# Band scores of two heads from one product over 128 partitions

## The chip, the cores and the metric

The kernel runs on one core of one Trainium2 chip. The metric is the device time of one launch in microseconds (us). An engine's name is shortened as in the profile: PE is TensorE (PEld its weight loads), DVE is VectorE, ACT is ScalarE, POOL is GpSimd and SP is SyncE, which issues most of the DMAs. Engines run their own instructions in order and wait for one another by semaphores.

## The reference

A local-global attention over 8 batches, 8 heads, 576 positions of 64 values, followed by a mixture of 16 experts on its output. The part that the change touches is the local attention: a position attends to the positions less than 4 away, a band of 7.

```python
def _attn_ref(q, k, v):
    B, H, S, D = q.shape                       # 8, 8, 576, 64
    factor = 4
    scale = 1.0 / np.sqrt(D)
    ...
    q_d = q.reshape(B, H, S // 4, factor, D).mean(axis=3)   # and k_d, v_d
    out_d = sm_attn(q_d, k_d, v_d)
    out_up = np.repeat(out_d, factor, axis=2)
    pos = np.arange(S)
    mask = np.abs(pos[:, None] - pos[None, :]) < factor
    scores = scale * np.matmul(q, k.transpose(0, 1, 3, 2))
    scores = np.where(mask, scores, -1000000000.0)
    scores = scores - np.max(scores, axis=-1, keepdims=True)
    attn = np.exp(scores)
    attn = attn / (np.sum(attn, axis=-1, keepdims=True) + 1e-09)
    out_local = np.matmul(attn, v)
    return (out_up + out_local).astype(np.float32)

def reference(**kwargs):
    ...
    attn_out = _attn_ref(**attn_kwargs)
    B, H, S, D = attn_out.shape
    x = np.ascontiguousarray(attn_out.transpose(0, 2, 1, 3)).reshape(B * S, H * D)
    return _moe_ref(x=x, **moe_kwargs)         # a group of 4, then an expert of 4 in it, for each token
```

## The kernel before

The attention works in 16 units. A unit is two heads of two batches: the 128 partitions hold the 64 values of the one head and the 64 of the other, and the free dimension holds the two batches and the positions. `load_k` (L177) and `load_q` (L181) bring them in that form, a DMA each on SP's queue, into `kt` (three buffers, made in `__init__`, L76) and `qT`; keys are padded by 3 positions at both ends on the host.

Band scores: 576 positions of a batch are 18 blocks of 32 queries, and a block sees 38 keys. `s_local` (L239) issues, for one head `h`, 36 float32 products (18 blocks of two batches): 64 partitions of that head, 32 queries as the stationary side, 38 keys as the moving side, into one of four column groups `j` and one of nine places `g` of a PSUM bank [128, 9, 38]. In the first three units (`EARLY_UNITS`) a bf16 product with the identity first puts the mask there. The profile shows two matmul records, and two weight loads, to a float32 product.

`s_local_out` (L256) then takes that bank, for one head: DVE adds the mask (L268) and takes the maximum per row (L269), POOL subtracts it (L270); in the first three units DVE takes the maximum (L265) and subtracts (L266). The result goes to `E` [128, 9, 48, 2], whose last index is the head. `s_local_exp` (L272) takes the exponential on ACT, again for one head. `soft_local_sum` and `soft_local` (both heads at once) divide by the sums; `turn_e` turns `E` for the product with the windows of values, `x_bank` (L419).

The global half reads the same `kt`: `pool_k` (L228) sums each four keys, on DVE with one reduction over [128, 2, 144, 4] or on POOL with three adds, as its step says, into `kd`; `pool_q` does the same for the queries. `s_down` (L290) multiplies them, and `s_down_max`, `s_down_exp`, `soft_down`, `turn_pd`, `out_down`, `turn_down`, `down_store` and `load_down` lead its result to the windows `vw`, from which `x_bank` adds both halves. PSUM for scores has three banks (pool `psd`), for the rest four (`ps`).

After the attention, logits and the router (`logits`, `choose`, `places`, `lists`, `ranks`) find each token's expert. One early expert is computed while the last units end; the others follow in `Experts.main`.

The order is written out by hand. `ORDER`, a string of steps such as `s_local 9 0` or `pool_k 7 P`, is run through in order, and each engine and each DMA queue gets its instructions in that order. Which engine takes a step with a choice is the step's last letter (D for DVE, P for POOL, A for ACT, S for SP). `pool_k` is on DVE in units 0, 1, 3, 5, 6, 8 and 10, on POOL in the nine others. The steps at the start are:

```
shared_rows; warm_up 12; masks; masks_out A; load_k 1; clear E 1; s_local 0 1; clear_windows 0; pool_q 0 D
pool_k 0 D; clear E 0; load_q 1; s_local 0 0; s_local_out 0 1; quarter_sum; clear vs 0; s_local_out 0 0; load_k 2
```

Before these stand the loads and memsets of `__init__`. `shared_rows` copies a pattern to two buffers on DVE (the copies have the helper's line, L161); `clear_windows` (L139) clears a buffer of `vw` on POOL, `clear` (L109) the rims of `E` (L114) and a part of `vs` (L116).

Of the kernel before, what the change touches and what calls it, by code (L numbers as in the profile page):

```python
# [9 lines left out]
F32 = mybir.dt.float32  # L10
# [4 lines left out]
ALU = mybir.AluOpType  # L15
AX = mybir.AxisListType
# [3 lines left out]
P = 128  # L20
B, H, S, D = 8, 8, 576, 64
SD = S // 4
G = 9
W = 38
WW = 48
LEAD = (WW - W) // 2
NBLK = 18
# [20 lines left out]

KEYS = (0, 112, 160)

TILES = (slice(0, P), slice(160, 160 + P), slice(112, 176))


class Attention:
# [9 lines left out]
    def __init__(self, tc, q, k, v, idf, xd, left, right, dram):  # L64
        nc = self.nc = tc.nc
        self.tc, self.q, self.k, self.idf = tc, q, k, idf
        n = NTOK * DM
        self.v, self.vm = v[0:n].rearrange("(b h s d) -> b h s d", h=H, s=S, d=D), v[n:].rearrange("(u p f) -> u p f", u=4 * NB, p=SD)
        cp = self.cp = left.enter_context(tc.tile_pool(name="attc", bufs=1))
        self.a1 = left.enter_context(tc.tile_pool(name="att1", bufs=1))  # L70
        self.a2 = left.enter_context(tc.tile_pool(name="att2", bufs=2))
        self.inp = right.enter_context(tc.tile_pool(name="inp", bufs=2, side="right"))
        self.odd = [dram.tile([320, P], F32, name=f"odd{i}") for i in range(2)]
        self.st, self.banks, self.lg = {}, {}, {}
        self.xd = xd
        self.kt = [self.inp.tile([P, 2, S + 6], F32, name=f"kt{i}", bufs=1) for i in range(3)]  # L76
        self.load_k(0)
        self.load_q(0)
        self.mask = self.inp.tile([P, G, W], BF16, name="mask", bufs=1)
        self.vw = [(cp.tile([P, 2 * NBLK, P], F32, name=f"vw{i}") if i < 2 else self.inp.tile([P, 2 * NBLK, P], F32, name="vw2", bufs=1)) for i in range(3)]  # L80
        self.warm = self.inp.tile([P, 4 * P], BF16, name="warm", bufs=1)
        nc.vector.memset(self.warm, 0.0)
        one = cp.tile([1, 1], F32, name="one")
        nc.gpsimd.memset(one, 0.0)
        nc.scalar.activation(one, one, AF.Exp)
        self.idb = cp.tile([P, P], BF16, name="idb")
        self.vd = [cp.tile([P, 3, 2, D], F32, name=f"vd{i}") for i in range(2)]
        self.vs = [self.inp.tile([P, 3, 2, 4 * D], F32, name=f"vs{i}", bufs=1) for i in range(3)]
        self.mg = [cp.tile([P, 5], F32, name=f"mg{i}") for i in range(2)]
        self.sg = [cp.tile([P, 5], F32, name=f"sg{i}") for i in range(2)]  # L90
        self.rg = [cp.tile([P, 6], F32, name=f"rg{i}") for i in range(2)]
        self.kept = {}
        for n, more, shape in (
            ("pt", 1, [P, G * P]), ("x", 2, [P, G, P]), ("PdT", 1, [P, 3, 2 * SD]), ("od", 1, [P, 2 * SD]), ("odn", 1, [P, 3, 2, D])
        ):
            self.kept[n] = [cp.tile(shape, F32, name=f"{n}0")] + [self.inp.tile(shape, F32, name=f"{n}{i + 1}", bufs=1) for i in range(more)]
        self.E = [cp.tile([P, G, WW, 2], F32, name=f"E{i}") for i in range(2)]
        self.xT = cp.tile([P, 27 * P // 2], F32, name="xT")
        self.edge = self.inp.tile([P, 3, W], F32, name="edge", bufs=1)
# [9 lines left out]
    def clear(self, what, i):  # L109

        memset = self.nc.gpsimd.memset
        if what == "E":
            for w in (slice(0, LEAD), slice(LEAD + W, WW)):
                memset(self.E[i][:, :, w], 0.0)  # L114
        elif what == "vs":
            memset(self.vs[i][:, 2], 0.0)  # L116

    def masks(self):

        nc = self.nc  # L120
        m, me = self.edge[:, 0], self.edge[:, 1:3]
        nc.gpsimd.memset(m, 0.0)
        for j in range(4):
            s = m[32 * j : 32 * j + 32]
            for sign, base in ((1, 0), (-1, 6)):
                nc.gpsimd.affine_select(out=s, in_=s, pattern=[[sign, W]], compare_op=ALU.is_ge, fill=-1e30, base=base, channel_multiplier=-sign)
        for i, (sign, base) in enumerate(((1, -3), (-1, 34))):
            nc.gpsimd.affine_select(out=me[:, i], in_=m, pattern=[[sign, W]], compare_op=ALU.is_ge, fill=-1e30, base=base, channel_multiplier=0)
# [45 lines left out]
            self.st[u] = {"h0": 2 * hp, "b0": 2 * bp}  # L174
        return self.st[u]

    def load_k(self, u):  # L177
        self.unit(u)
        self.nc.sync.dma_start(out=self.kt[u % 3], in_=self.k[u])

    def load_q(self, u):  # L181
        s = self.unit(u)
# [43 lines left out]
    def pool_k(self, u, eng):  # L226
        s = self.st[u]
        kd = s["kd"] = self.inp.tile([P, 2, SD], F32, tag="kd", name=f"kd{u}")  # L228
        x = self.kt[u % 3][:, :, 3 : 3 + S].rearrange("p b (s t) -> p b s t", t=4)
        if eng == "D":  # L230
            self.nc.vector.tensor_reduce(out=kd, in_=x, axis=AX.X, op=ALU.add)
        else:
            self.add4(kd, [x[:, :, :, t] for t in range(4)])

    def pool_v(self, u):
        x = self.vs[u % 3].rearrange("p k b (t d) -> p k b t d", t=4)
        self.add4(self.vd[u % 2], [x[:, :, :, t] for t in range(4)])

    def s_local(self, u, h):  # L239

        nc = self.nc
        s = self.st[u]
        pt = self.bank(("s", h), u, [P, G, W], True)
        early = u < EARLY_UNITS
        if early:
            nc.tensor.matmul(pt.rearrange("p g w -> p (g w)"), self.idb, self.mask.rearrange("p g w -> p (g w)"), start=True, stop=False, skip_group_check=True)
        r = slice(64 * h, 64 * h + 64)
        for lin in range(2 * NBLK):
            g, j = divmod(lin, 4)
            b, blk = divmod(lin, NBLK)  # L250
            nc.tensor.matmul(
                pt[32 * j : 32 * j + 32, g], s["qT"][r, b, 32 * blk : 32 * blk + 32], self.kt[u % 3][r, b, 32 * blk : 32 * blk + W], start=not early, stop=True,
                skip_group_check=True,
            )

    def s_local_out(self, u, h):  # L256
        nc = self.nc
        s = self.st[u]
        pt = self.banks.pop((("s", h), u))
        if "ml" not in s:  # L260
            s["ml"] = self.a2.tile([P, G, 2], F32, tag="ml", name=f"ml{u}")
            s["sl"] = self.a2.tile([P, G, 2], F32, tag="sl", name=f"sl{u}")
        m, e = s["ml"][:, :, h], self.E[u % 2][:, :, LEAD : LEAD + W, h]
        if u < EARLY_UNITS:
            nc.vector.tensor_reduce(out=m, in_=pt, axis=AX.X, op=ALU.max)  # L265
            nc.vector.tensor_tensor(out=e, in0=pt, in1=m.unsqueeze(2).to_broadcast([P, G, W]), op=ALU.subtract)  # L266
        else:
            nc.vector.tensor_tensor(out=e, in0=pt, in1=self.mask, op=ALU.add)  # L268
            nc.vector.tensor_reduce(out=m, in_=e, axis=AX.X, op=ALU.max)  # L269
            nc.gpsimd.tensor_tensor(out=e, in0=e, in1=m.unsqueeze(2).to_broadcast([P, G, W]), op=ALU.subtract)  # L270

    def s_local_exp(self, u, h):  # L272
        e = self.E[u % 2][:, :, LEAD : LEAD + W, h]
        self.nc.scalar.activation(e, e, AF.Exp, scale=SCALE)

    def vec(self, e):
# [114 lines left out]
    def turn_down(self, u):  # L391
        pt = self.bank("odt", u, [P, 3, P])
        for c, q in enumerate(TILES):
            n = q.stop - q.start
# [810 lines left out]
shared_rows; warm_up 12; masks; masks_out A; load_k 1; clear E 1; s_local 0 1; clear_windows 0; pool_q 0 D  # L1205
pool_k 0 D; clear E 0; load_q 1; s_local 0 0; s_local_out 0 1; quarter_sum; clear vs 0; s_local_out 0 0; load_k 2
load_q 2; pool_q 1 P; load_v 0; s_down 0; warm_up 6; s_down_max 0; s_local_exp 0 1; s_down_exp 0 0; s_local_exp 0 0; s_down_exp 0 2
s_down_exp 0 1; pool_q 2 D; pool_k 1 D; s_local 1 1; clear_windows 1; s_local_out 1 1; s_local 1 0; clear vs 2; turn_pd 0 0
soft_local_sum 0 D; turn_pd 0 2; s_local_out 1 0; load_k 3; turn_pd 0 1; turn_pd_out 0 1 A; turn_pd_out 0 0 A; soft_local 0
turn_pd_out 0 2 A; s_down 1; s_local_exp 1 0; pool_v 0; out_down 0; s_local_exp 1 1; turn_e 0 0; s_down_max 1; clear vs 1  # L1210
turn_e 0 2; s_down_exp 1 0; soft_down 0 P; s_down_exp 1 1; load_windows 0; turn_e 0 1; soft_local_sum 1 D; turn_e_out 0 2 A
# [214 lines left out]
```

## Time and profile before

| | us |
|---|---|
| three timed runs | 752.67, 755.56, 758.88 |
| their median | 755.56 |
| the profiled execution | 760.53 |
| its span, first to last instruction | 758.7 |
| PE busy | 701.6 |
| DVE busy | 462.4 |
| ACT busy | 362.7 |
| POOL busy | 266.0 |

The busy times are sums over the whole span; the mean granted clock of TensorE was 0.964. Matmuls overlap, so a mean duration of one is longer than its share of the time. A row of the profile names the line, the engine, the operation and "output<-inputs"; "idle before, releaser" is the time in which the engine had nothing to run before these instructions, and what ended it. "issue" means that the engine waited for nothing that the profile shows.

### The profile page before, as it was taken

The page shows a single profiled execution, that of the slowest core. Times are in us where ns is not written, and L with a number is a line of the kernel's source. Part 1 is how long each engine was busy: PE and PEld are TensorE (multiplying, and loading weights), DVE is VectorE, ACT ScalarE, POOL GpSimd, SP SyncE. Part 2 cuts the span into 40 slices and gives each one's busy share as a digit, 9 for nine tenths or more (in the row PEclk, how much of TensorE's full clock was granted, in tenths as well). Part 3 has the DMA queues.
Part 4 walks back from the last instruction along what each step waited for, and adds up shares of the span by engine and source line. Part 5 has one row for each costly group of instructions (what it writes and reads, how often), then busy time and mean ns, then how long its engine had stood idle before and what let it go on. Part 6 is the DMA issues. An engine that isn't in the chain of part 4 may idle for free. (4 is left out here: it accounts for less than half of the span.)

```text
span 758.7 us, 19970 instructions
## 1 busy us (share of the span) xinstructions
PE 701.6 (92%) x8132; PEld 638.7 (84%) x8133; DVE 462.4 (61%) x834; ACT 362.7 (48%) x797; POOL 266.0 (35%) x307
## 2 busy tenths in 40 slices
PE   7788878897887878999999999999999999999996
PEld 4666757686665767999899999999999999999985
DVE  7877775898685583764545454555555555565541
ACT  3436534665564423654445444444545455555531
POOL 8966664676462552102130312203113113212211
PEclk9889998999989999999999999999999999999999
DMA  8779899789869535674463555555556556656600
GB/s 296 249 193 282 239 265 278 219 219 255 214 163 256 156 111 165 212 228 167 153 191 115 191 175 172 185 168 193 188 190 204 184 193 210 202 201 195 220 26 25
DMA packets 158243, 146.94 MB, mean 194 GB/s; under 512 B 69396, under 2 KB 129812, under 8 KB 158148
## 3 DMA queue, kind: packets, MB, share of 16 engines
q1 hardware_dynamic: 133540, 115.11, 50.8%
q0 software_dynamic: 7088, 21.66, 8.2%
q10 hardware_dynamic: 17520, 8.85, 4.4%
q8 instruction: 65, 1.06, 0.6%
q14 instruction: 30, 0.25, 0.1%
HBM read 124.29 MB, written 22.29 MB: 193 GB/s over the span
## 5 line engine op out<-in xcount | busy, mean ns | idle before, releaser
L863 PE MATMUL ph<-xh,w1h 128*128 128x256 f32 (+13 forms) x512 | 162.3, 318 | 0.0
L834 POOL DMA_INDIRECT xg<-xd,gi x47 | 48.5, 1032 | 319.1 <-ACT yo L937 289.7
L863 PE MATMUL ph<-xl,w1h 128*128 128x256 f32 (+13 forms) x512 | 157.0, 308 | 0.0
L863 PE MATMUL ph<-xh,w1l 128*128 128x256 f32 (+13 forms) x512 | 156.8, 308 | 0.0
L822 DVE TENSOR_TENSOR w2l<-raww,w2h 128x1024 fp32r<-128x1024 f32 x61 | 74.6, 1224 | 73.7 <-ACT w2h L821 61.1
L911 PE MATMUL y<-hl,w2h 128*128 128x416 f32 (+11 forms) x384 | 115.3, 311 | 0.0
L911 PE MATMUL y<-hh,w2l 128*128 128x416 f32 (+11 forms) x384 | 114.3, 308 | 0.0
L821 ACT ACTIVATE w2h<-raww 128x1024 fp32r<-128x1024 f32 x64 | 67.6, 1057 | 74.2 <-PE y L911 54.1
L863 PEld LDWEIGHTS ph<-xh,w1h 128*128 128x128 f32 x512 | 97.3, 190 | 1.5 <-issue 0.2
L863 PEld LDWEIGHTS ph<-xl,w1h 128*128 128x128 f32 x512 | 97.5, 191 | 1.0
L822 DVE TENSOR_TENSOR w1l<-raww,w1h 128x1024 fp32r<-128x1024 f32 x60 | 73.4, 1224 | 39.5 <-ACT w1h L821 34.6
L863 PEld LDWEIGHTS ph<-xh,w1l 128*128 128x128 f32 x512 | 97.2, 190 | 0.3
L868 DVE SCALAR_TENSOR_TENSOR hl<-ph,hh 128x256 fp32r<-128x256 f32 (+13 forms) x128 | 60.4, 476 | 55.7 <-ACT hh L867 49.1
L867 ACT ACTIVATE hh<-ph 128x256 fp32r<-128x256 f32 (+13 forms) x128 | 53.8, 421 | 76.2 <-PE ph L863 72.3
L911 PE MATMUL y<-hh,w2h 128*128 128x416 f32 (+11 forms) x384 | 87.7, 312 | 0.0
L821 ACT ACTIVATE w1h<-raww 128x1024 fp32r<-128x1024 f32 x64 | 67.5, 1056 | 32.7 <-PE ph L863 23.0
L938 POOL DMA_INDIRECT out_dram<-yo,oi x47 | 48.1, 1023 | 73.0 <-ACT yo L937 41.5
L911 PEld LDWEIGHTS y<-hh,w2l 128*128 128x128 f32 x384 | 72.3, 188 | 0.1
L911 PEld LDWEIGHTS y<-hl,w2h 128*128 128x128 f32 x384 | 72.2, 188 | 0.2
L911 PEld LDWEIGHTS y<-hh,w2h 128*128 128x128 f32 x384 | 62.9, 188 | 0.1
L424 PE MATMUL b_x<-vw,pt 128*32 128x128 f32 x1152 | 43.5, 301 | 10.3 <-ACT xT L159 4.5
L424 PEld LDWEIGHTS b_x<-vw,pt 128*32 128x32 f32 x1152 | 34.1, 120 | 16.0 <-issue 9.6
(223 smaller groups left out, 1272.1 us busy)
## 6 DMA issues: line engine op xcount, KB each, us to landing
raww<-in_moe_w_dram SPq DMA_DIRECT2D x128, 512.0 KB, 4.6
vw<-in_v_dram SPq DMA_DIRECT2D x62, 216.0 KB, 5.8
kt<-in_k_dram SPq DMA_DIRECT2D x16, 582.0 KB, 4.8
qT<-in_q_dram SPq DMA_DIRECT2D x16, 576.0 KB, 6.0
xd<-x ACTq DMA_DIRECT2D x15, 576.0 KB, 6.3
vs<-in_v_dram SPq DMA_DIRECT2D x16, 512.0 KB, 7.1
vw<-odd SPq DMA_DIRECT2D x16, 144.0 KB
odd<-odn SPq DMA_DIRECT2D x16, 128.0 KB
```

The source lines that it names most:

```text
L424: self.nc.tensor.matmul(pt[32 * j : 32 * j + 32, t], self.of("pt", u)[:, 32 * lin : 32 * lin + 32], self.windows(u)[:, lin], start=True, s ...
L821: self.nc.scalar.activation(hi, raw, AF.Copy)
L822: eng.tensor_tensor(out=lo, in0=raw, in1=hi.bitcast(F32), op=ALU.subtract)
L834: self.nc.gpsimd.indirect_dma_start(out=xg[:w], out_offset=None, in_=self.xd[0:rows], in_offset=bass.IndirectOffsetOnAxis(ap=st["gi"][:w, ...
L863: nc.tensor.matmul(ph, a[:, k, cs], st[b][:, k], start=(n == 0), stop=(n == 11))
L867: nc.scalar.activation(hh, ph, AF.Relu)
L868: nc.vector.scalar_tensor_tensor(out=hl, in0=ph, scalar=0.0, in1=hh.bitcast(F32), op0=ALU.max, op1=ALU.subtract)
L911: nc.tensor.matmul(y, a[:, f % 2, cs], b, start=(f == 0 and n == 0), stop=(f == 7 and n == 2))
L938: i = nc.gpsimd.indirect_dma_start(out=self.out, out_offset=bass.IndirectOffsetOnAxis(ap=oi, axis=0), in_=yo[:m], in_offset=None, bounds_c ...
```

## The change

The two heads' keys no longer lie in the same columns. `kt` gets an index more: [128, 2, 2, 582], partitions, head, batch, position. Head 0's keys lie in partitions 0 to 63 of place 0, head 1's in partitions 64 to 127 of place 1; the other halves of both places are zero, and are cleared once. One product over all 128 partitions, with the 32 queries of both heads as the stationary side and 2 x 38 columns of keys as the moving side, then gives the scores of both heads of a block beside each other.

So `s_local` no longer goes by heads but by `BANDS`: call 0 takes the blocks of places 0 to 4 (20 products), call 1 of places 5 to 8 (16 products), with PSUM tiles [128, 5, 2, 38] and [128, 4, 2, 38]. `s_local_out` and `s_local_exp` follow. `load_k` becomes two DMAs of 64 partitions; for the first unit the second is issued by ACT. `pool_k` becomes two instructions (or twice three) of 64 partitions. Two of the three buffers are cleared on DVE in `__init__`, the third by a new step, `clear kt 2`, on POOL. The rest of `ORDER` stays.

```diff
+BANDS = ((0, 5), (5, 4))
...
-        self.kt = [self.inp.tile([P, 2, S + 6], F32, name=f"kt{i}", bufs=1) for i in range(3)]
-        self.load_k(0)
+        self.kt = [self.inp.tile([P, 2, 2, S + 6], F32, name=f"kt{i}", bufs=1) for i in range(3)]
+        self.load_k(0, "A")
...
         nc.vector.memset(self.warm, 0.0)
+        for i in range(2):
+            self.clear_keys(i, nc.vector)
...
+        else:
+            self.clear_keys(i, self.nc.gpsimd)
+
+    def clear_keys(self, i, eng):
+        for h in range(2):
+            eng.memset(self.kt[i][64 * h : 64 * h + 64, 1 - h], 0.0)
...
-        self.nc.sync.dma_start(out=self.kt[u % 3], in_=self.k[u])
+        for h in range(2):
+            r = slice(64 * h, 64 * h + 64)
+            self.queue("S" if h == 0 else second).dma_start(out=self.kt[u % 3][r, h], in_=self.k[u, r])
...
-        x = self.kt[u % 3][:, :, 3 : 3 + S].rearrange("p b (s t) -> p b s t", t=4)
-        if eng == "D":
-            self.nc.vector.tensor_reduce(out=kd, in_=x, axis=AX.X, op=ALU.add)
-        else:
-            self.add4(kd, [x[:, :, :, t] for t in range(4)])
+        for h in range(2):
+            r = slice(64 * h, 64 * h + 64)
+            x = self.kt[u % 3][r, h, :, 3 : 3 + S].rearrange("p b (s t) -> p b s t", t=4)
+            if eng == "D":
+                self.nc.vector.tensor_reduce(out=kd[r], in_=x, axis=AX.X, op=ALU.add)
+            else:
+                self.add4(kd[r], [x[:, :, :, t] for t in range(4)])
...
-    def s_local(self, u, h):
+    def s_local(self, u, i):
...
-        pt = self.bank(("s", h), u, [P, G, W], True)
+        g0, n = BANDS[i]
+        pt = self.bank(("s", i), u, [P, n, 2, W], True)
...
-        r = slice(64 * h, 64 * h + 64)
-        for lin in range(2 * NBLK):
+        for lin in range(4 * g0, 4 * (g0 + n)):
             g, j = divmod(lin, 4)
             b, blk = divmod(lin, NBLK)
             nc.tensor.matmul(
-                pt[32 * j : 32 * j + 32, g], s["qT"][r, b, 32 * blk : 32 * blk + 32], self.kt[u % 3][r, b, 32 * blk : 32 * blk + W], start=not early, stop=True,
+                pt[32 * j : 32 * j + 32, g - g0], s["qT"][:, b, 32 * blk : 32 * blk + 32], self.kt[u % 3][:, :, b, 32 * blk : 32 * blk + W], start=not early, stop=True,
...
-        m, e = s["ml"][:, :, h], self.E[u % 2][:, :, LEAD : LEAD + W, h]
+        shape = [P, n, 2, W]
+        m, e = s["ml"][:, g0 : g0 + n], self.band(u, i).rearrange("p g w h -> p g h w")
+        mb = m.unsqueeze(3).to_broadcast(shape)
...
-            nc.vector.tensor_tensor(out=e, in0=pt, in1=self.mask, op=ALU.add)
+            nc.vector.tensor_tensor(out=e, in0=pt, in1=self.mask[:, g0 : g0 + n].unsqueeze(2).to_broadcast(shape), op=ALU.add)
             nc.vector.tensor_reduce(out=m, in_=e, axis=AX.X, op=ALU.max)
-            nc.gpsimd.tensor_tensor(out=e, in0=e, in1=m.unsqueeze(2).to_broadcast([P, G, W]), op=ALU.subtract)
+            nc.gpsimd.tensor_tensor(out=e, in0=e, in1=mb, op=ALU.subtract)
...
-s_down_exp 0 1; pool_q 2 D; pool_k 1 D; s_local 1 1; clear_windows 1; s_local_out 1 1; s_local 1 0; clear vs 2; turn_pd 0 0
+s_down_exp 0 1; pool_q 2 D; pool_k 1 D; s_local 1 1; clear_windows 1; s_local_out 1 1; s_local 1 0; clear vs 2; clear kt 2; turn_pd 0 0
```

More of the change, by code (lines that the diff above doesn't have):

```diff
@@ L175, in unit, with load_k @@
         return self.st[u]
-    def load_k(self, u):
+    def load_k(self, u, second="S"):
         self.unit(u)
-        self.nc.sync.dma_start(out=self.kt[u % 3], in_=self.k[u])
+        for h in range(2):
+            r = slice(64 * h, 64 * h + 64)
+            self.queue("S" if h == 0 else second).dma_start(out=self.kt[u % 3][r, h], in_=self.k[u, r])
     def load_q(self, u):
@@ L237, in pool_v @@
         self.add4(self.vd[u % 2], [x[:, :, :, t] for t in range(4)])
-    def s_local(self, u, h):
+    def s_local(self, u, i):
         nc = self.nc
         s = self.st[u]
-        pt = self.bank(("s", h), u, [P, G, W], True)
+        g0, n = BANDS[i]
+        pt = self.bank(("s", i), u, [P, n, 2, W], True)
         early = u < EARLY_UNITS
         if early:
-            nc.tensor.matmul(pt.rearrange("p g w -> p (g w)"), self.idb, self.mask.rearrange("p g w -> p (g w)"), start=True, stop=False, skip_group_check=True)
-        r = slice(64 * h, 64 * h + 64)
-        for lin in range(2 * NBLK):
+            mask = self.mask[:, g0 : g0 + n].unsqueeze(2).to_broadcast([P, n, 2, W])
+            nc.tensor.matmul(pt, self.idb, mask, start=True, stop=False, skip_group_check=True)
+        for lin in range(4 * g0, 4 * (g0 + n)):
             g, j = divmod(lin, 4)
@@ L251, in s_local, with band, s_local_out @@
             nc.tensor.matmul(
-                pt[32 * j : 32 * j + 32, g], s["qT"][r, b, 32 * blk : 32 * blk + 32], self.kt[u % 3][r, b, 32 * blk : 32 * blk + W], start=not early, stop=True,
+                pt[32 * j : 32 * j + 32, g - g0], s["qT"][:, b, 32 * blk : 32 * blk + 32], self.kt[u % 3][:, :, b, 32 * blk : 32 * blk + W], start=not early, stop=True,
                 skip_group_check=True,
             )
-    def s_local_out(self, u, h):
+    def band(self, u, i):
+        g0, n = BANDS[i]
+        return self.E[u % 2][:, g0 : g0 + n, LEAD : LEAD + W]
+    def s_local_out(self, u, i):
         nc = self.nc
         s = self.st[u]
-        pt = self.banks.pop((("s", h), u))
+        g0, n = BANDS[i]
+        pt = self.banks.pop((("s", i), u))
         if "ml" not in s:
@@ L262, in s_local_out, with s_local_exp @@
             s["sl"] = self.a2.tile([P, G, 2], F32, tag="sl", name=f"sl{u}")
-        m, e = s["ml"][:, :, h], self.E[u % 2][:, :, LEAD : LEAD + W, h]
+        shape = [P, n, 2, W]
+        m, e = s["ml"][:, g0 : g0 + n], self.band(u, i).rearrange("p g w h -> p g h w")
+        mb = m.unsqueeze(3).to_broadcast(shape)
         if u < EARLY_UNITS:
             nc.vector.tensor_reduce(out=m, in_=pt, axis=AX.X, op=ALU.max)
-            nc.vector.tensor_tensor(out=e, in0=pt, in1=m.unsqueeze(2).to_broadcast([P, G, W]), op=ALU.subtract)
+            nc.vector.tensor_tensor(out=e, in0=pt, in1=mb, op=ALU.subtract)
         else:
-            nc.vector.tensor_tensor(out=e, in0=pt, in1=self.mask, op=ALU.add)
+            nc.vector.tensor_tensor(out=e, in0=pt, in1=self.mask[:, g0 : g0 + n].unsqueeze(2).to_broadcast(shape), op=ALU.add)
             nc.vector.tensor_reduce(out=m, in_=e, axis=AX.X, op=ALU.max)
-            nc.gpsimd.tensor_tensor(out=e, in0=e, in1=m.unsqueeze(2).to_broadcast([P, G, W]), op=ALU.subtract)
-    def s_local_exp(self, u, h):
-        e = self.E[u % 2][:, :, LEAD : LEAD + W, h]
+            nc.gpsimd.tensor_tensor(out=e, in0=e, in1=mb, op=ALU.subtract)
+    def s_local_exp(self, u, i):
+        e = self.band(u, i)
         self.nc.scalar.activation(e, e, AF.Exp, scale=SCALE)
```

## The prediction

> **What bounds the kernel now.** I read the page's first line and the table of windows first, then the waits, then the timeline of each engine around the touched steps. The columns of a window row are its length, busy time (and instructions) of PE, PEld, DVE, ACT and POOL, the granted clock, the DMA share and GB/s.
>
> ```profile
> span 758.7 us, 19970 instructions
> ...
> 0.00:45.00 45.00, 32.72 (x769) 22.95 (x774) 33.25 (x64) 17.99 (x64) 38.71 (x70) 0.90 0.77 255
> 45.00:140.00 95.00, 81.88 (x2030) 64.58 (x2022) 70.07 (x158) 48.40 (x161) 53.70 (x60) 0.92 0.91 247
> 140.00:200.00 60.00, 53.97 (x1305) 43.01 (x1305) 54.46 (x116) 37.03 (x119) 43.01 (x60) 0.94 0.89 233
> 200.00:300.00 100.00, 80.88 (x951) 66.82 (x952) 60.00 (x159) 40.44 (x104) 44.30 (x34) 0.90 0.64 180
> 300.00:758.00 458.00, 452.17 (x3093) 441.36 (x3091) 244.61 (x341) 218.82 (x353) 86.27 (x84) 1.00 0.54 175
> ```
>
> From 300 us on PE is busy 452 of 458 us: the experts run at the pace of TensorE, and nothing the change touches lies there. So what counts is by how much the attention, the first 300 us, ends earlier or later. There the bound changes hands: POOL is the fullest in the first 45 us (38.7), PE to 140 (81.9 of 95), DVE and PE together to 200 (54.5 and 54.0 of 60).
>
> ```profile
> POOL E L270 <- DVE ml L269: 38.7, 13, 9.2
> ACT x L159 <- PE b_x L424: 20.7, 18, 5.4
> ...
> PE b_s L251 <- issue: 8.5, 7, 2.6
> ```
>
> In the waits of the attention (sum, times, longest), POOL waits for DVE and ACT for PE. PE's largest own wait stands in front of the band products themselves, and it is for nothing that the profile shows.
>
> **The change, part by part. The products.** A unit issued 72 products (144 records, two to a product); now 36, each with 76 columns in place of 38.
>
> ```profile
> 38.41 0.69 PE L251 MATMUL b_s<-kt,qT 64*32 64x38 f32 x54
> 41.66 0.36 PE L251 MATMUL b_s<-kt,qT 64*32 64x38 f32 x18 [2.56 <-issue]
> ...
> 52.50 1.47 PE L251 MATMUL b_s<-kt,qT 64*32 64x38 f32 x144
> ...
> 55.11 2.17 PE L424 MATMUL b_x<-vw,pt 128*32 128x128 f32 x72
> ```
>
> The two calls of a unit took 1.47 us, 10.2 ns a record of 38 columns; `x_bank`, which has the new shape on the stationary side (128 rows, 32 columns), took 2.17/72 = 30.1 ns a record of 128 columns. That is nearly proportional to columns, and the columns of a unit stay the same: 144 x 38 = 72 x 76. On the line through both rows a record of 76 costs 18.6 ns, so 72 x 18.6 = 1.34 us: 0.13 us less a unit, **-2.1 us** over 16. The bounds are no gain (0) and a price that is all fixed (0.73 a unit, -11.7); the line is between two measured shapes, so I take it.
>
> [...]
>
> **The instructions.** A call is cut at 38.41: 54 records, then 2.56 us of nothing, then the other 18. A semaphore is no cause in mid-call.
>
> ```profile
> q8 instruction: 65, 1.06, 0.6%
> ```
>
> Instructions come in packets of 1.06 MB/65 = 16 KB, and the band products with their weight loads are the quickest to use them up: 288 instructions in 1.47 us, now 144 in 1.34. My reading is that the 8.5 us of stalls are a late packet. The bounds are 0 and -8.5. Half as many instructions go through at about half the rate, so most should go, but a packet border then falls elsewhere and some stalls lie beside a DVE that is late anyway: I take half, **-4.3**.
>
> **The start.** DVE gets four memsets of 64 partitions x 1164 elements before anything else, POOL two (`clear kt 2`).
>
> ```profile
> 0.94 0.27 DVE L82 MEMSET warm<- 128x256 uint32 x1 [0.94 <-PEq L1399]
> 2.19 1.46 DVE L161 COPY pt<-shared 32x1152 f32<-32x1152 f32 x2 [0.97 <-POOL shared L153]
> 5.95 3.95 POOL L139 MEMSET vw<- 128x4608 f32 x1
> 8.52 0.51 DVE L265 TENSOR_REDUCE ml<-b_s 128x9 f32<-128x342 f32 x1
> 12.48 1.35 DVE L216 TENSOR_REDUCE qd<-qT 128x288 f32<-128x1152 f32 x1 [0.74 <-DMA qT<-in_q_dram]
> 14.36 3.96 POOL L139 MEMSET vw<- 128x4608 f32 x1
> 16.87 1.94 DVE L283 TENSOR_SCALAR sl<-sl 128x18 f32<-128x18 f32 x1
> 20.28 0.48 PE L297 MATMUL b_d<-kd,qd 64*32 64x144 f32 x12 [2.71 <-DVE E L266]
> 22.44 2.40 PE L384 MATMUL b_od<-PdT,vd 128*64 128x144 f32 x16 [1.68 <-POOL vd L224]
> ...
> 62.40 0.18 DVE L283 TENSOR_SCALAR sl<-sl 128x18 f32<-128x18 f32 x1
> ```
>
> At 0.27/256 us an element a memset costs 1.23, the four end near 6.1, and the copies of `shared_rows` (1.46) come behind them instead of at 2.19. By then POOL clears `vw` until 9.9. The tensor_scalar of 16.87 shows what such a clear does: 1.94 us in place of 0.18, until POOL's memset at 14.36 was over. If the copies are held so, they run 9.9 to 11.4, `pool_q` (1.3) and the doubled `pool_k` (2.6) end at 15.3, and the first `s_local_out` comes 6.8 us after its old 8.52; if not held, 3.0 after. Then the second `pool_k` adds 1.3, DVE's 0.74 wait for a load goes, and so does the 1.76 hold at 16.87: +5.6 (or +1.8) at the subtract for which PE waits at 20.28. Two steps on PE waited 1.68 for POOL's `vd`, which takes in part of that: +3.9. POOL's two clears, at 3.95/4608 us an element 2.0 together, put `vd` 2.0 later, which is the lower end. I take **+3.9**, ends +2.0 and +6.8.
>
> Whether a copy is held as a tensor_scalar is, no row shows. [...]
>
> **`pool_k`.** A reduction, or three adds, over 128 partitions become two, or six, over 64 each, with as many elements per partition.
>
> ```profile
> L231 DVE TENSOR_REDUCE kd<-kt 128x288 f32<-128x1152 f32 x7 | 9.4, 1344 | 0.0
> L222 POOL TENSOR_TENSOR kd<-kt 128x288 f32<-128x288 f32 x9 | 7.6, 847 | 0.2
> L223 POOL TENSOR_TENSOR kd<-kd,kt 128x288 f32<-128x288 f32 x9 | 8.5, 947 | 0.7
> L224 POOL TENSOR_TENSOR kd<-kd,kt 128x288 f32<-128x288 f32 x9 | 8.5, 947 | 0.7
> L126 POOL TENSOR_SCALAR_AFFINE_SELECT edge<-edge 32x38 f32<-32x38 f32 x8 | 2.5, 313 | 0.5
> L283 DVE TENSOR_SCALAR sl<-sl 128x18 f32<-128x18 f32 x14 | 6.7, 481 | 0.5
> ```
>
> The bounds for an instruction on half the partitions are half the price (nothing added) and the same price. An instruction on 32 partitions took 313 ns for 38 elements, so few partitions are not cheap: I take the same price. DVE pays 1.34 more in units 0, 1 (counted), 3, 5, 6, 8 and 10; POOL 0.85 + 0.95 + 0.95 = 2.74 more in units 2, 4, 7, 9 and 11 to 15, 24.7 in all.
>
> ```profile
> 42.53 0.42 DVE L403 TENSOR_TENSOR odn<-b_odt,rg 128x256 f32<-128x256 f32 x1 [2.65 <-PE b_odt L395]
> 54.01 0.52 DVE L268 TENSOR_TENSOR E<-b_s,mask 128x342 f32<-128x342 f32 x1 [0.43 <-PE b_s L251]
> 78.36 0.46 DVE L161 COPY PdT<-b_pd 128x288 f32<-128x288 f32 x1 [1.86 <-PE b_pd L363]
> 95.45 0.52 DVE L268 TENSOR_TENSOR E<-b_s,mask 128x342 f32<-128x342 f32 x1 [0.68 <-PE b_s L251]
> 128.95 0.56 DVE L161 COPY x<-b_x 128x384 f32<-128x384 f32 x1 [2.54 <-PE b_x L424]
> ...
> 155.27 2.26 POOL L270 TENSOR_TENSOR E<-E,ml 128x342 f32<-128x342 f32 x2 [1.49 <-DVE ml L269]
> 165.24 1.68 POOL L270 TENSOR_TENSOR E<-E,ml 128x342 f32<-128x342 f32 x2 [1.70 <-DVE ml L269]
> ```
>
> These are DVE's next waits behind units 3, 5, 6, 8 and 10. Three cover the 1.34; of the other two 0.9 and 0.7 stay: **+1.6** (ends 0 and 6.7). On POOL units 11 and 12 come close together, before subtracts that had waited 1.49 and 1.70; the exponentials and DVE's sums queue behind those: 5.48 - 3.19 = **+2.3** (ends 0 and 5.5). The other units have longer waits or the first 45 us behind them.
>
> The last one meets PE:
>
> ```profile
> 217.18 0.94 POOL L224 TENSOR_TENSOR kd<-kd,kt 128x288 f32<-128x288 f32 x1
> 219.46 1.17 PE L297 MATMUL b_d<-kd,qd 64*128 64x144 f32 x20
> ```
>
> Unit 15's keys, ready at 218.1, would be ready at 220.9, and PE would start `s_down 15` 1.4 later with the router's chain behind it: **+1.4** (ends 0 and 2.7).
>
> A busier POOL also holds DVE's small instructions more: the group of L283 lost 14 x 0.30 = 4.2 us in this way with POOL busy 180 of 300; 27 us more would add 0.6, and the like for its neighbours: **+1.0** (0 to 2).
>
> **What is costed at nothing.** DVE's and ACT's band steps keep their elements (2 x 342 = 380 + 304); if the extra dimension in POOL's subtract costs, it falls under the +2.3. Two half loads of `kt` move the same bytes:
>
> ```profile
> kt<-in_k_dram SPq DMA_DIRECT2D x16, 582.0 KB, 4.8
> ```
>
> The order loads keys a unit or two ahead of use, which covers a second issue and even a landing of twice 4.8 us; without that lead each unit would pay it.
>
> **The sum.** -2.1 - 4.3 + 3.9 + 1.6 + 2.3 + 1.4 + 1.0 = +3.8 us. The profiled execution took 760.5 us (span 758.7, 1.8 around it), so 764.3 on its terms; it was 5.0 above the median of the three timed runs, 755.56, on which I state 759.4.
>
> **The rivals.** Faster: the instruction supply was the true brake. All 8.5 us go, DVE and POOL have room for the halves (they waited, in the rows above), the start costs its lower end: -2.1 - 8.5 + 2.0 = -8.6, 747.0. For it speaks that everyone waits for PE; against it that DVE was 91% busy from 140 to 200. Chance 0.13.
>
> Slower: DVE becomes the bound of the whole attention because the hold at 6.1 us is never won back. The 6.8 and the five 1.34 (6.7) count in full, PE's gain hides, and stalls give back 2: 6.8 + 6.7 + 2.3 + 1.4 + 1.0 - 2.0 = +16.2, 771.8. It decides once DVE's waits for PE, such as the 2.65 and 1.86, are gone in the new trace. Chance 0.22.
>
> A fixed price per product: 0.73 a unit saved in place of 0.13, 759.4 - 9.6 = 749.8. The near proportionality of 10.2 and 30.1 ns speaks against it: 0.05.
>
> The change does not do what it says: 76 columns over all rows cost twice 38 and the stalls remain, 759.4 + 2.1 + 4.3 = 765.8. Chance 0.11.
>
> **How the numbers follow.** My forecast has 0.49. A change of under 1% (748.0 to 763.1) is about what a measurement of this kernel cannot tell from none; forecast and fixed price lie there: 0.54. Faster 0.13, slower 0.22 + 0.11 = 0.33. The range goes to the centres of the two outer rivals, 747 to 772.
>
> **What would show it.** Right: 72 records a unit in about 1.34 us; fewer and shorter issue waits in front of `b_s`; the copies of L161 ending near 11.4 and the first band maximum near 15.3; `kd` reductions of 64 partitions at 1.34 us; PE waiting for `kd` before the last `s_down`. Wrong: copies that run during POOL's clear, half-priced `kd` instructions, or issue stalls that only move to other lines. If experts start earlier than before, the start term or the stall term was misjudged.

## The result

The changed kernel takes 762.79 us in the median (759.25 to 768.38), the kernel before on the same chip 755.21 (747.72 to 760.45). The ratio is 1.0113, with a 95% interval of 1.0074 to 1.0151: 8.5 us slower by the ratio (5.6 to 11.4), where the prediction had 3.8. The profiled executions can't show this sum: that of before took 760.5 us, above its kernel's median, and that of after 759.25 (span 757.4), the least of its kernel's times. So what follows compares places, and sums come from the timed runs.

The table of windows of the changed kernel, with the columns of the one shown of before:

```profile
0.00:45.00 45.00, 30.85 (x413) 20.69 (x415) 39.92 (x58) 16.29 (x59) 38.82 (x69) 0.74 0.88 234
45.00:140.00 95.00, 80.22 (x1533) 61.84 (x1535) 78.91 (x168) 48.32 (x162) 66.91 (x74) 0.94 0.98 247
140.00:200.00 60.00, 52.80 (x1025) 41.75 (x1021) 55.12 (x119) 36.90 (x120) 53.67 (x72) 0.97 0.99 239
200.00:300.00 100.00, 84.36 (x938) 68.00 (x938) 66.14 (x165) 42.24 (x109) 48.40 (x38) 0.90 0.65 186
```

PE runs far fewer instructions (413 in place of 769 in the first row, 1533 in place of 2030 in the second) in nearly the same busy time. DVE is fuller (78.9 of 95 us, before 70.1), and so is POOL (66.9, before 53.7). The column before the last is one that I passed over in the prediction: the DMA share goes from 0.91 to 0.98 and from 0.89 to 0.99 in the two middle rows, while the bytes per second (247; 239 against 233) hardly rise. The transfer engines are busier with the same bytes.

The groups of the changed kernel that answer to the price list of the prediction, by line and form (busy time, mean ns of one | idle time before, and what ended it):

```profile
L267 PE MATMUL b_s<-kt,qT 128*32 128x76 f32 x1152 | 28.3, 250 | 4.8 <-DMA qT<-in_q_dram 3.6 <-ACT Pd L354 1.3
L246 DVE TENSOR_REDUCE kd<-kt 64x288 f32<-64x1152 f32 x14 | 20.5, 1468 | 0.3
L235 POOL TENSOR_TENSOR kd<-kt 64x288 f32<-64x288 f32 x18 | 15.4, 858 | 0.8
L236 POOL TENSOR_TENSOR kd<-kd,kt 64x288 f32<-64x288 f32 x18 | 17.6, 976 | 1.4
L237 POOL TENSOR_TENSOR kd<-kd,kt 64x288 f32<-64x288 f32 x18 | 17.7, 986 | 1.4
```

A `pool_k` instruction on 64 partitions costs what one on 128 did (847 and 947 ns on POOL before, 858, 976 and 986 now; on DVE the median of one is 1349 ns, before 1343), so DVE pays 20.5 us in place of 9.4 and POOL 50.7 in place of 24.6. The means on POOL take in a few instructions that were held up; the medians are 828, 939 and 943 ns, before 835, 946 and 944. The band products no longer wait for "issue" on PE. Their weight loads still do, for 13.1 us in place of 18.4:

```profile
PEld b_s L267 <- issue: 13.1, 22, 4.2
```

The start, in the timelines of DVE and of POOL:

```profile
5.34 1.03 DVE L126 MEMSET kt<- 64x1164 f32 x1 [0.28 <-issue]
6.38 4.25 DVE L171 COPY pt<-shared 32x1152 f32<-32x1152 f32 x2
...
14.68 0.47 DVE L288 TENSOR_REDUCE ml<-b_s 128x8 f32<-128x304 f32 x1
...
18.19 4.57 DVE L345 TENSOR_SCALAR mg<-mg 128x5 f32<-128x5 f32 x1
```

```profile
5.16 3.95 POOL L149 MEMSET vw<- 128x4608 f32 x1
...
17.32 3.94 POOL L149 MEMSET vw<- 128x4608 f32 x1
```

The copies of `shared_rows` last 4.25 us in place of 1.46: POOL's memset of 5.16 ends at 9.1, and they end 1.5 us behind it, at 10.6, as forecast. Then comes a hold that I had not foreseen: the delay carries the scaling of `mg`, 0.17 us before, into POOL's second clear, and it lasts 4.57. So a copy is held by POOL's clear (4.25 us) as the tensor_scalar of 16.87 was (1.94 us), which no row of before had shown. Unit 1's band products start at 24.08 us (before 12.96).

### The profile page after: what moved, and what is told of

Its sections match the earlier page's. It is cut to its first block, busy times and chain, and to the rows that moved or that the text cites. A ratio compares the mean times of both kernels' runs of the same rounds, so it can differ in the third digit from the quotient of the medians.

```text
span 757.4 us, 17750 instructions
## 1 busy us (share of the span) xinstructions
PE 698.7 (92%) x6980; PEld 632.1 (83%) x6981; DVE 483.0 (64%) x845; ACT 361.3 (48%) x797; POOL 294.2 (39%) x336
## 5 line engine op out<-in xcount | busy, mean ns | idle before, releaser
L845 DVE TENSOR_TENSOR w2l<-raww,w2h 128x1024 fp32r<-128x1024 f32 x61 | 74.6, 1224 | 73.4 <-ACT w2h L844 62.9
L845 DVE TENSOR_TENSOR w1l<-raww,w1h 128x1024 fp32r<-128x1024 f32 x60 | 73.4, 1224 | 38.9 <-ACT w1h L844 31.9
L844 ACT ACTIVATE w1h<-raww 128x1024 fp32r<-128x1024 f32 x64 | 67.5, 1057 | 32.1 <-PE ph L886 24.6
L447 PEld LDWEIGHTS b_x<-vw,pt 128*32 128x32 f32 x1152 | 33.4, 119 | 18.5 <-issue 11.4
```

Source lines behind the costliest of these rows:

```text
L447: self.nc.tensor.matmul(pt[32 * j : 32 * j + 32, t], self.of("pt", u)[:, 32 * lin : 32 * lin + 32], self.windows(u)[:, lin], start=True, s ...
L844: self.nc.scalar.activation(hi, raw, AF.Copy)
L845: eng.tensor_tensor(out=lo, in0=raw, in1=hi.bitcast(F32), op=ALU.subtract)
```

## The experiments

The theory after the result was: the start and the halves of `pool_k` cost more than forecast, and the products give part back. The first four runs put the costs into the kernel before, one at a time and together, and took the start out of the changed one.

**The memsets alone.** The kernel before, with:

```diff
+        self.spare = [self.inp.tile([P, 2, S + 6], F32, name=f"spare{i}", bufs=1) for i in range(3)]
+        for i in range(2):
+            self.clear_spare(i, nc.vector)
...
+    def clear_spare(self, i, eng):
+        for h in range(2):
+            eng.memset(self.spare[i][64 * h : 64 * h + 64], 0.0)
```

> The kernel before with nothing but the six key memsets of the change, written to spare tiles that nobody reads: four on DVE ahead of the copies of shared_rows, two on POOL at the place of the new step. Theory (the loss has two parts, the start and pool_k): the copies and then the scaling of mg are held under POOL's two clears of vw as in the changed kernel, unit 1's band scores start 8 to 11 us later and the kernel is about 4 us slower, ratio 1.005. Rival (pool_k is the whole loss): the delay of the start is won back by the end of the attention, ratio 1.000 (within 0.3%).

Measured: ratio 1.0108 (1.0051 to 1.0165), 8.1 us. The start is not won back. The size is double what the theory gave it and above the prediction's upper end of 6.8, though the interval (3.8 to 12.4 us) holds both. In its trace the scaling of `mg` starts at 16.77 and lasts 3.19, and unit 1's band products start at 21.31, 8.4 us late, as expected.

**`pool_k` alone.** The kernel before, with the new `pool_k` on its own layout:

```diff
-        x = self.kt[u % 3][:, :, 3 : 3 + S].rearrange("p b (s t) -> p b s t", t=4)
+        for h in range(2):
+            r = slice(64 * h, 64 * h + 64)
+            x = self.kt[u % 3][r, :, 3 : 3 + S].rearrange("p b (s t) -> p b s t", t=4)
```

> The kernel before with nothing but pool_k cut into two instructions of 64 partitions (twice three on POOL). Theory: DVE pays 1.34 us more in each of 7 units and POOL 2.74 us in each of 9, of which 5 to 6 us reach the end (the prediction's 1.6 + 2.3 + 1.4 for it, and 1.3 at the start): ratio 1.007. Rival (pool_k is the whole loss): ratio 1.011 or more. Rival (it is hidden and the start is the whole loss): 1.000.

Measured: ratio 1.0155 (1.0098 to 1.0212), 11.7 us. This lies above the theory's 1.007 and looks like the rival's; but the memsets cost as well, so neither is the whole. In its trace the scaling of `mg` comes at 13.38 and is not held (0.17 us); PE waits 1.2 us for "issue" in front of the band products (before 8.5), and the reduction that reads the ranks comes 8.2 us later than before. So this loss is not one of late instructions.

**All costs, without the products.** Both edits and the halved loads of the third experiment below:

> The kernel before with all that the change adds and without its products: the six memsets to spare tiles, pool_k in halves, and keys loaded by two transfers of 64 partitions. Theory: 10 to 12 us slower than before, ratio 1.014 to 1.016, that is 3 to 4 us slower than the changed kernel (1.0113), because the products over 128 partitions give that much back; PE still waits some 8 us for nothing that the profile shows in front of the band products. Rival (the products gain nothing): the ratio of the changed kernel, 1.011. Rival (the new products cost time): below 1.008.

Measured: ratio 1.0367 (1.0305 to 1.0429), 27.7 us. The changed kernel, which has these costs and the new products, loses 8.5. So, if the costs weigh the same beside the new products, these give back about 27.7 - 8.5 = 19 us (the two intervals together give 14 to 25), three times the 6.4 of the prediction. What they do away with stands in the timeline of PE in this run (start, length, [idle time before, releaser]), and in its waits (sum, times, longest):

```profile
36.04 1.11 PE L264 MATMUL b_s<-kt,qT 64*32 64x38 f32 x57 [3.48 <-issue]
...
51.74 0.34 PE L264 MATMUL b_s<-kt,qT 64*32 64x38 f32 x16 [3.86 <-issue]
```

```profile
PEld b_s L264 <- issue: 28.6, 26, 4.0
PE b_s L264 <- issue: 24.2, 9, 3.9
```

The cut of a call 18 records before its end, at 41.66 in the kernel before with 2.56 us, is here again at 51.74 with 3.86 and 16 records: the same place in the list of instructions but for two records, at another time. PE's waits of this kind have grown from 8.5 to 24.2 us, and in the changed kernel they are gone. That is near the 19 us.

That these waits are late instructions the record of the transfers shows. In the kernel before, a packet of 16 KB on the instruction queue q8 landed at 40.16, and the cut call goes on at 41.66; in this run packets landed at 34.64 and 50.12, and the calls go on at 36.04 and 51.74. Of the waits of PE for "issue" of 0.8 us and more in the attention, each one in both kernels (7 and 10) ended 1.3 to 1.8 us after such a landing. In the 2 us in which the call of the kernel before breaks off, from 38 to 40, the transfer engines were fully busy (a share of 1.02).

**The quiet start.** The changed kernel, with the clears of buffers 1 and 2 on ACT, which is idle there:

```diff
-        for i in range(2):
-            self.clear_keys(i, nc.vector)
+        self.clear_keys(0, nc.vector)
...
+    def zero_keys(self, i):
+        for h in range(2):
+            r = slice(64 * h, 64 * h + 64)
+            self.evac("A", self.kt[i][r, 1 - h].rearrange("p b s -> p (b s)"), self.warm[r, 0:1].to_broadcast([64, 2 * S + 12]))
...
-shared_rows; warm_up 12; masks; masks_out A; load_k 1; clear E 1; s_local 0 1; clear_windows 0; pool_q 0 D
+shared_rows; warm_up 12; masks; masks_out A; zero_keys 1; zero_keys 2; load_k 1; clear E 1; s_local 0 1; clear_windows 0; pool_q 0 D
```

> The changed kernel with the clears of key buffers 1 and 2 taken from DVE and POOL to ACT, as copies of a zero column between its mask copies and its first exponential; DVE clears buffer 0 alone. Theory: the copies of shared_rows end by 5.6 us, the first band maximum comes near 10 and not 14.7, the scaling of mg is not held, and 4 to 5 us of the loss go: ratio 1.005 to 1.006. Rival (pool_k is the whole loss): the start gets earlier but the ratio stays at 1.011.

DVE's timeline of this run:

```profile
3.76 1.45 DVE L175 COPY pt<-shared 32x1152 f32<-32x1152 f32 x2
...
11.79 0.47 DVE L292 TENSOR_REDUCE ml<-b_s 128x8 f32<-128x304 f32 x1
...
15.11 4.07 DVE L349 TENSOR_SCALAR mg<-mg 128x5 f32<-128x5 f32 x1
```

Measured: ratio 1.0035 (1.0000 to 1.0070), some 6 us better than 1.0113. The copies take 1.45 us again and end at 5.2; but the first maximum came at 11.8 and not near 10, for `pool_q` waited for its transfer until 7.77, and the scaling of `mg` is still held for 4.07 us. So the second and the third expectation failed, and the start isn't yet free.

The sum of the memsets and `pool_k` alone, 1.08 + 1.55 = 2.6%, leaves 1.0% of the 3.67 for the halved loads, if costs add up; the prediction had costed them at nothing.

**The halved loads alone, cut by heads and cut by batch.** Two kernels: the one before with the change's `load_k`, and the same with two transfers that each keep all 128 partitions:

```diff
-        self.nc.sync.dma_start(out=self.kt[u % 3], in_=self.k[u])
+        for h in range(2):
+            r = slice(64 * h, 64 * h + 64)
+            self.queue("S" if h == 0 else second).dma_start(out=self.kt[u % 3][r], in_=self.k[u, r])
```

```diff
-        self.nc.sync.dma_start(out=self.kt[u % 3], in_=self.k[u])
+        for b in range(2):
+            self.queue("S" if b == 0 else second).dma_start(out=self.kt[u % 3][:, b], in_=self.k[u, :, b])
```

> The kernel before with nothing but its keys loaded by two transfers of 64 partitions. The kernel with all three costs was 3.67% slower, the memsets alone 1.08% and pool_k alone 1.55%, so 1.0% is left over. Theory A (the half loads cost it): ratio 1.008 to 1.012, and in the trace PE and its weight loads wait longer for issue in front of the band products than the 26.9 us of before. Theory B (the costs add up worse together than alone, the loads are free): ratio 1.000, within 0.4%.

> The kernel before with its keys loaded by two transfers as in b_load, but cut by batch: each has all 128 partitions and half the bytes of a row. The cut by heads (64 partitions each) made the kernel 1.6% slower (0.76 to 2.43%). Theory (64 partitions take a transfer only half as fast, so the engines of the DMA are busier and everything behind them is later): ratio 1.000 to 1.005, and the share of time of the transfer queues stays near before's 55.2% (q1 and q10 together). Rival (the second issue and its landing cost it): ratio 1.012 or more with this cut too.

Measured: by heads 1.0160 (1.0076 to 1.0243), by batch 1.0017 (0.9987 to 1.0048). It is not the second issue or the second landing that costs, but the 64 partitions. The queues of the page (packets, MB, share of the time of 16 engines), first of before, then by heads, then by batch:

```profile
q1 hardware_dynamic: 133540, 115.11, 50.8%
...
q10 hardware_dynamic: 17520, 8.85, 4.4%
```

```profile
q1 hardware_dynamic: 133716, 114.82, 52.3%
...
q10 hardware_dynamic: 17600, 9.15, 4.6%
```

```profile
q1 hardware_dynamic: 135700, 114.82, 51.7%
...
q10 hardware_dynamic: 17664, 9.15, 4.6%
```

The MB are the same (123.96 or 123.97 together). Times the spans, the engines worked 55.2% of 758.7 = 419 us, 56.9% of 769.8 = 438 and 56.3% of 751.3 = 423: 19 us more by heads, 0.6 us for each of the 32 half loads, and 4 by batch. That these are "only half as fast" is not shown: at the mean of before, 419 us for 123.96 MB, 291 KB take some 1.0 us, and 0.6 more makes about 0.6 of that rate, an estimate. Nor does a run show why 64 partitions keep the engines longer.

These transfers also hit PE through its instructions: its wait for issue in front of the band products rose from 8.5 us to the value in the waits of the run by heads.

```profile
PE b_s L253 <- issue: 15.6, 7, 3.5
```

By batch it was 8.4. But most of the loss by heads arises at one place, and it is that of the memsets. Lines of before, then by heads:

```profile
5.99 1.35 DVE L216 TENSOR_REDUCE qd<-qT 128x288 f32<-128x1152 f32 x1 [2.34 <-DMA qT<-in_q_dram]
11.57 0.17 DVE L322 TENSOR_SCALAR mg<-mg 128x5 f32<-128x5 f32 x1
12.96 0.54 PE L251 MATMUL b_s<-kt,qT 64*32 64x38 f32 x36
```

```profile
7.48 1.35 DVE L218 TENSOR_REDUCE qd<-qT 128x288 f32<-128x1152 f32 x1 [3.83 <-DMA qT<-in_q_dram]
13.58 5.20 DVE L324 TENSOR_SCALAR mg<-mg 128x5 f32<-128x5 f32 x1
14.36 3.94 POOL L139 MEMSET vw<- 128x4608 f32 x1
20.14 1.37 PE L253 MATMUL b_s<-kt,qT 64*32 64x38 f32 x72
289.49 1.13 DVE L749 TENSOR_REDUCE rv<-sel 128x60 f32<-128x960 f32 x1
```

The first queries land later, `mg` comes 2.0 us later and lasts 5.20, until POOL's clears are over at 18.8, and unit 1's band products start 7.2 us late. At the reduction that reads the ranks (289.49, before 279.11) the delay is 10.4 us, so some 7 of it were lost in the first 20 us and not unit by unit. By batch `mg` comes at 11.94 and takes 0.44. The margin is small: with `pool_k` alone `mg` came at 13.38, 0.2 us before the one here, and was not held. So the memsets alone and the half loads alone each run into the same hold, and their costs can't be added: the three alone make 8.1 + 11.7 + 12.1 = 31.9 us, all together 27.7.

**Is it the count of instructions?** The changed kernel with the quiet start, and in front of each band product of units 3 to 15 one of a single column, whose place the band product overwrites:

```diff
+            if not early:
+                nc.tensor.matmul(
+                    pt[32 * j : 32 * j + 32, g - g0, 0, 0:1], s["qT"][:, b, 32 * blk : 32 * blk + 32], self.kt[u % 3][:, 0, b, 32 * blk : 32 * blk + 1], start=True, stop=True,
+                    skip_group_check=True,
+                )
```

> The changed kernel with its quiet start, and in units 3 to 15 a product of one column in front of each of the 36 band products, into a place that the band product then overwrites: the instruction count of before (144 matmul records and 144 weight loads a unit) at hardly more columns. Theory (what the products gave back is instruction supply): waits for issue in front of the band products come back, from some 7 to over 20 us in PE and its weight loads together, at packet borders in mid-call, and the ratio goes from 1.0035 to 1.015 or more. Rival (the gain lies in the work of the products): the calls get longer by at most 0.73 us a unit, most of it beside a DVE that is later anyway, waits for issue stay near 7 us, ratio 1.003 to 1.010.

Measured: ratio 1.0196 (1.0133 to 1.0260), 1.6% above the quiet start, some 12 us. What PE and its weight loads waited for in front of the products, in the view of the tile `b_s`, first with the quiet start, then with the added products (the execution profiled here took 781.3 us against a median of 772.18, so it is read for the kind of wait more than for its size):

```profile
  issue: 6.7, 20
```

```profile
  issue: 19.0, 22
```

The waits came back nearly to the theory's 20. But a unit's two calls also got longer, in unit 4 from 1.39 us to 2.03, 13 x 0.64 = 8.3 us if nothing covers it. The ratio lies above the rival's 1.010; how much of the 12 us is waits and how much PE's added work, this run can't say.

**What `pool_k` costs beside the new products.** The quiet start, with:

```diff
-        for h in range(2):
-            r = slice(64 * h, 64 * h + 64)
-            x = self.kt[u % 3][r, h, :, 3 : 3 + S].rearrange("p b (s t) -> p b s t", t=4)
+        x = self.kt[u % 3][:, 0, :, 3 : 3 + S].rearrange("p b (s t) -> p b s t", t=4)
```

> The changed kernel with its quiet start, and pool_k one instruction (or three) over all 128 partitions of place 0: the pooled keys of the second head are left out (they are zeros). Theory: the second halves cost 5 to 8 us here as in the kernel before, so the ratio falls from 1.0035 to 0.993 to 0.997. Rival (with the new products they are hidden): 1.003.

Measured: ratio 0.9991 (0.9950 to 1.0032), 0.44% or 3.3 us below the quiet start, and the intervals overlap. It is under the 5 to 8 us expected, and far under the 11.7 that the same halves cost in the kernel before. Its profiled execution is 7.1 us ahead of the quiet start's at the reduction that reads the ranks (270.79 against 277.88), in part because `mg` is not held (0.52 us), and loses 5.0 of them behind it. So the 3.3 us are no price of the halves alone.

**Two repairs that failed.** The quiet start with 11 evacuations moved to ACT (`x_bank_out 2 1 D` became `x_bank_out 2 1 A`, and so on), and with the second half load of every unit on ACT's queue:

```diff
-    def load_k(self, u, second="S"):
+    def load_k(self, u, second="A"):
```

> The changed kernel with its quiet start, and 11 evacuations of PSUM of units 0 to 5 on ACT in place of DVE, 0.5 us each, where DVE hardly has an idle stretch (50 to 90 us). Theory (there DVE has become the bound): 3 to 5 us less, ratio 0.997 to 1.000. Rival (the order waits for PE or transfers there): no difference from 1.0035, or more where ACT's exponentials come later.

> The changed kernel with its quiet start, and the second head's half load of every unit issued by ACT in place of SP, so that the two halves stand in two queues. Theory (the halves of 64 partitions are slow one behind the other, and together as fast as one of 128): 3 to 6 us less than with the quiet start alone, ratio 0.996 to 1.000. Rival (they cost by their second issue): 16 more issues of 0.57 us lie on ACT and none is won, ratio 1.003 to 1.010.

Measured: 1.0102 (1.0033 to 1.0172) and 1.0106 (1.0062 to 1.0149). Neither theory held. The moved evacuations took DVE from 80.6 to 74.6 us between 45 and 140 without an earlier end, so a full DVE alone isn't the brake there. Two queues side by side didn't make 64 partitions as fast as 128: the queues worked 59.0% of 763.4 = 450 us, with the quiet start alone 57.7% of 754.1 = 435. With two queues unit 0's band products came at 9.56, for the queries landed later, and with the quiet start alone at 7.89; whether that is all of why this version came out slower I leave open.

**The products without the costs.** Keys are loaded dense by one transfer, `pool_k` reads them there with whole instructions, and copies of 64 partitions spread them beside zeros for the band products:

```diff
+        self.kn = [self.inp.tile([P, 2, S + 6], F32, name=f"kn{i}", bufs=1) for i in range(3)]
...
+    def spread(self, u, *engines):
+        for h, e in enumerate(engines):
+            r = slice(64 * h, 64 * h + 64)
+            self.evac(e, self.kt[u % 2][r, h], self.kn[u % 3][r])
...
+        self.nc.sync.dma_start(out=self.kn[u % 3], in_=self.k[u])
...
+        x = self.kn[u % 3][:, :, 3 : 3 + S].rearrange("p b (s t) -> p b s t", t=4)
```

> The new products without the other two costs: keys are loaded dense, as before, by one transfer over 128 partitions, pool_k is one instruction (or three) over 128 partitions of the dense keys, and a copy of 64 partitions on ACT (head 0) and one on POOL (head 1; ACT in units 0 and 1) spread them to two buffers with places beside zeros, some 24 steps ahead of the band products; the clears are those of the quiet start. Theory (halved loads and halved pool_k are the loss, the products with half the instructions a gain): the 9.3 us of pool_k's second halves on DVE and the slow loads go for 1.18 us a unit on ACT and about as much on POOL: ratio 0.985 to 0.997, waits for issue in front of the band products under 12 us. Rival (the copies put as much back, on engines with an order of their own): 1.000 to 1.010.

> The same as a_dense with both copies on ACT in every unit, 2.4 us a unit in place of 1.2, and none on POOL. If ACT has the room that its waits for PE promise: as a_dense within 0.4%. If ACT's chain of evacuations and exponentials is the brake: 0.5 to 1.0% slower than a_dense.

Measured: 0.9934 (0.9905 to 0.9963) with one copy on ACT and one on POOL, 0.9992 (0.9957 to 1.0028) with both on ACT. The first beats both kernels; it is 0.7% or 5.0 us faster than the one before. Both copies on ACT came out 0.6% slower than that, which is what was expected if ACT's chain is the brake; but the two intervals touch. The groups of the first for the copies (count, then min/median/max ns), and PE and its weight loads in the waits:

```profile
L179 ACT ACTIVATE kt<-kn x18: 1156/1166/1185, 7.2 to 191.8; 64x1164 f32<-64x1164 f32 x18
L183 POOL COPY kt<-kn x14: 1152/1152/1675, 19.1 to 189.3; 64x1164 f32<-64x1164 f32 x14
```

```profile
PE b_s L272 <- issue: 0.3, 1, 0.3
PEld b_s L272 <- issue: 11.1, 21, 4.9
```

A unit pays 1.17 us on each of the two for the copies, and is freed of the second half of `pool_k`, of the half loads and of half the products' instructions. PE waits only 0.3 us for issue in front of the band products. The reduction that reads the ranks after the attention (DVE's timeline), first of before, then of after, of the run with all costs, and of this one:

```profile
279.11 1.13 DVE L747 TENSOR_REDUCE rv<-sel 128x60 f32<-128x960 f32 x1
```

```profile
278.13 1.13 DVE L770 TENSOR_REDUCE rv<-sel 128x60 f32<-128x960 f32 x1
```

```profile
302.33 1.13 DVE L760 TENSOR_REDUCE rv<-sel 128x60 f32<-128x960 f32 x1
```

```profile
273.42 1.13 DVE L775 TENSOR_REDUCE rv<-sel 128x60 f32<-128x960 f32 x1
```

Against before the three runs are 1.0 us earlier, 23.2 later and 5.7 earlier at that point, in the attention, where the prediction said that it must count. But their spans differ from that of before by -1.3, +19.0 and -10.3 us. So what follows that point is not fixed, as the prediction took it to be: from there to the end the executions of the first two kernels take 479.6 and 479.3 us, those of the other two 475.3 and 475.0. What makes these 4 us is open.

## Why the prediction came near, and where its steps failed

The direction and the range held, but not because the terms were right: costs and gain were both about a third of what the runs showed, and the errors cancelled. That was luck. In us, with the terms of the prediction beside the runs that have each part alone in the kernel before (they overlap, for the memsets and the half loads run into the same hold):

| part | predicted | measured |
|---|---|---|
| products and instructions | -6.4 | about -19 (14 to 25), all costs against the changed kernel |
| start | +3.9 (2.0 to 6.8) | +8.1 (3.8 to 12.4); 6 won by the quiet start |
| `pool_k`, its first part counted under the start | +5.3, and 1.0 for DVE held by POOL | +11.7 (7.4 to 16.0); 3.3 beside the new products |
| halved loads | 0 | +12.1 (5.8 to 18.4) |
| all costs | +10.2 | +27.7 (23.0 to 32.3) |

- **The products' own time.** The line through two rows gave 1.34 us a unit; where the 72 records ran without a break it measured 1.39 to 1.41, in one unit 1.54. That gain over 1.47 is some 1 us in all. The fixed price per product is refuted: 1.39 us for 72 records are 19.3 ns each, where the 144 of before followed each other every 10.2.
- **The instructions.** The reading of the stalls as late packets held: they end 1.3 to 1.8 us after a packet lands, and the new products rid PE of them. The step that failed is "The bounds are 0 and -8.5": it took the stalls of before for the most that there was to win, but the change's own costs would have raised them, as they did to 24.2 us with the old products. A term that removes a stall was sized without the terms that feed it.
- **The start.** The hold of the copies was right in place and kind (ends 10.6 us, forecast 11.4; first maximum 14.7, forecast 15.3). Mis-sized was the sentence that "the 1.76 hold at 16.87" goes away: a hold of 4.4 us more at `mg` took its place, because the delayed DVE met the next clear of POOL. No run shows the cover of 1.68 us by PE's wait for `vd` that the term counted on: unit 1's scaling of `mg`, right behind the step in question, came 8.2 us later (30.7 against 22.5), not 3.9.
- **`pool_k`.** The price of half the partitions was right to 1% in the medians. What reached the end was mis-sized for the kernel before, where the halves cost 11.7 us; beside the new products 3.3 is less than the sum given. Waits of the trace of before were taken as cover one by one; they are not independent.
- **The loads.** "Two half loads of `kt` move the same bytes" is the step that was wrong in kind. The bytes are the same and the time isn't, 0.6 us more of all the engines for each. The lead of a unit or two covers a later landing of keys; it doesn't cover what else stands in line for the same engines: the first queries, which at the start have no lead, and instructions. The queries, with the hold of `mg` that follows, make some 7 of the 10.4 us in the trace by heads.
- **The rivals.** "The instruction supply was the true brake" had the mechanism that moved most, and still lost, as the costs were larger. "DVE becomes the bound" isn't borne out by the experiment that freed it. "The change does not do what it says" is false: stalls and half the records went.

## What to carry to other kernels

A packing that doubles the work of one product is paid by whoever else reads the packed data: load and reduce it dense over all partitions, and spread it with a copy just for the product that needs it (0.9934 against 1.0113). A transfer of the same bytes can cost more on fewer partitions (1.0160 in halves of 64, 1.0017 in halves of 128), and with the transfer engines as busy as here (shares of 0.91 and 0.89 before, from 45 to 200 us) a slow one was paid by what stands behind it, the first queries and PE's instructions. Where a change delays the start, look for the next instruction that the delay carries into another engine's long clear: here 2 us of delay became 7. And two costs that run into the same hold can't be measured alone and added.

## What the runs showed that was not expected

Instruction supply held PE in this kernel of small float32 products: 24.2 us of waits in the run with all costs, none in front of the same scores with half the instructions. The packets on the instruction queue have 16 KB each (65 and 1.06 MB before), and their transfer isn't hidden: a call breaks off while the transfer engines are fully busy (1.02 at the cut of before), and the waits end 1.3 to 1.8 us after the next packet lands.

The granted clock is part of the loss at the start. The stretch from 10 to 20 us in the windows, first of before, then of after (the clock is third from the end):

```profile
10.00:20.00 10.00, 6.44 (x187) 4.52 (x185) 9.06 (x15) 4.00 (x17) 9.50 (x14) 1.00 0.92 263
```

```profile
10.00:20.00 10.00, 7.29 (x90) 4.72 (x84) 9.56 (x14) 0.46 (x1) 6.78 (x9) 0.50 1.03 262
```

PE's timeline has unit 0's two calls, of the changed kernel and with the quiet start:

```profile
9.50 1.24 PE L267 MATMUL b_s<-kt,qT 128*32 128x76 f32 x32 [3.03 <-DMA qT<-in_q_dram]
...
11.11 1.49 PE L267 MATMUL b_s<-kt,qT 128*32 128x76 f32 x40
```

```profile
7.89 0.73 PE L271 MATMUL b_s<-kt,qT 128*32 128x76 f32 x32 [0.39 <-DMA qT<-in_q_dram]
...
8.82 0.86 PE L271 MATMUL b_s<-kt,qT 128*32 128x76 f32 x40
```

After a wait of 3.03 us for the queries the same records took 1.24 and 1.49 us, after one of 0.39 they took 0.73 and 0.86. The clock stood at 0.50 there too in the runs with the loads cut by heads, with all costs, and with two queues. Over the whole span its mean was 0.964 before, 0.960 after, 0.943 by heads, 0.944 with all costs and 0.970 with the dense keys, so it is below that of before in the three slower kernels and above it in the faster one. How much of each loss is the clock's, and how far the clock follows from PE's waits, no run here separates.
